# A new order of every engine's steps: the first MLP rows and the taps of k change places

## The chip, the cores and the metric

The kernel runs on one core of one Trainium2 chip. Its time is the device time of one execution in microseconds. Each kernel is run several times, and the median is given with the lowest and highest.

The core has five engines with a queue each, and an engine works through its own queue in order: TensorE (PE, matmuls and transposes into PSUM; PEld is its weight load), VectorE (DVE), ScalarE (ACT), GpSimd (POOL) and SyncE (SP), which issues all DMAs here. They wait for each other through semaphores.

## The reference

The inputs are bf16, with S = 2048 rows and D = 640 columns. The row x = `q` goes through two branches, which a gate mixes:

```
g = sigmoid((x * gate_w).sum(-1))

# branch A: a short convolution along the rows (4 taps), then a long one (FFT of length 2S)
k_shift[s] = sum_t k[s - 3 + t] * shift_k[:, 3 - t]
kv = k_shift * v
y  = irfft(rfft(kv padded to 2S) * rfft(ssm_k padded to 2S))[:S]
a  = x * (y + kv * ssm_D)

# branch B: an MLP that shifts quarters of its hidden columns along the rows, and a second MLP
h  = gelu(layernorm(x) @ w1)                      # 640 -> 640
hs = four column quarters of h, shifted by +1, -1, +2, -2 rows, @ w2
x1 = x + hs
b  = x1 + gelu(layernorm(x1) @ w3) @ w4           # 640 -> 1536 -> 640

out = g * a + (1 - g) * b
```

## The kernel before, in words

Row s lies in partition s // 16 at place s % 16, so each of the 16 places t1 is a tile of 128 rows. Rows are loaded in four quarters c of four places each.

**Branch A.** The taps of the short convolution are matmuls (`tap`, line 534): k is needed transposed (KT, channels on partitions), and a tap step multiplies slices of KT with diagonal matrices DG (line 494, built from `shift_k`) into PSUM. There are ten tap steps: `tap.0` to `tap.4` make places 0 to 7 for the five column blocks, `tap.5` to `tap.9` places 8 to 15. A tap step takes two PSUM buffers, and each half is multiplied with v in place (KV), either by VectorE from PSUM (line 548) or by a ScalarE copy (line 542) and then VectorE (line 545). So a tap needs the quarters of k and of v of its half; the first half also needs the last three places of quarter 3 turned by a partition (KW, `k_wrap`).
A quarter of k reaches KT in one of two ways, chosen in `k_load`: loaded plainly (line 507) and transposed by TensorE in 20 pieces (line 562) with copies out of PSUM by ScalarE (line 320) or VectorE (line 322), or brought by a transposing DMA on SP (line 503, the letter D).
The long convolution is a four-step Fourier transform: `step1` (lines 369 and 372) transforms KV, and the filter HT0 that `h_transpose` (lines 343, 346) makes, in eight column blocks each; copies go through a staging tile to DRAM (S_x, S_h, line 384). `gather` (line 391) reads them back in another layout, `step2` (line 413) makes the spectra XS and hs, `product` (lines 434 to 442, VectorE) multiplies them, `step3` (line 456) starts the inverse, and its copies gs go to DRAM (S_g, line 466). `gin` (line 480) reads them back, and `step4` (line 817) ends the inverse and multiplies with q and the gate (lines 821 to 831).

**Branch B.** `x_stats` (lines 620 to 636) takes mean and variance, on VectorE or ScalarE by a letter; `x_norm` (lines 603, 605) normalises; `x_turn` transposes the result, by TensorE (line 562) or by a DMA (line 593); `mlp1` (line 651) is the product with w1, its GELU (line 654) leaves PSUM into HT, and `h_shift` shifts rows. `w2` (line 728) and line 730 make x1, and line 733 its squares; `x1_norm` normalises again and transposes by DMA (line 755); `w3` (line 776), its GELU (line 781), `w4` (line 794) and line 796 end the branch. `scale_x1` (lines 300 and 302) multiplies x1 with 1 - g.

**What sets the order.** Nothing is scheduled by the compiler. `ORDER` is one long list, written out in the source, of some thousand entries `step.arguments:part`; `emit` calls them one after the other, and each part appends its instructions to the queues of its engines. A string such as `AAVVA` in an entry says, part by part, whether ScalarE (A) or VectorE (V) takes the work that either can do; D stands for a DMA transpose. Buffers come from rings of fixed size: four PSUM buffers for taps, transposes and the Fourier steps (psc), two for the MLPs (psm), four for rows in SBUF (tag row), two for transposed rows (tag xt). An instruction waits where its buffer's last reader has not finished. A DMA also waits until the eighth DMA before it has landed, since eight semaphores go round (an X load, ninth or tenth in the queue, waits for the first or second).

Line numbers below line 833 differ by three between the two kernels, because the list is three lines shorter; all lines named here lie above it.

Of the kernel before, what the change touches and what calls it, by code (L numbers as in the profile page):

```python
# [41 lines left out]
def kernel(  # L42
# [760 lines left out]
    def step4(t1, ev):  # L803
# [26 lines left out]
        def total():  # L830
# [5 lines left out]
        "open.L1.left:0 open.A2.right:0 kv_alloc:0 load_x0.0:0 consts0:0 load_x0.1:0 k_load.1.A:0 consts0:1 "  # L836
        "k_load.3.A:0 f1_table:0 load_cj:0 k_load.2.A:0 load_x.1:0 f4_table:0 v_load.3:0 f1_table:1 v_load.2:0 "
        "load_x.3:0 x_stats.0.VVVA:0 f4_table:1 x_stats.0.VVVA:1 load_w1:0 k_load.1.A:1 f1_table:2 x_stats.0.VVVA:2 "
        "x_stats.0.VVVA:3 z_cols:0 k_load.1.A:3 k_load.1.A:2 load_gw:0 k_load.1.A:5 x_stats.0.VVVA:4 k_load.3.A:1 "
        "load_h.4:0 k_load.1.A:4 kv_consts:0 k_load.3.A:3 k_load.1.A:6 k_load.3.A:2 k_load.3.A:5 k_load.0.D:0 "  # L840
        "k_load.2.A:1 k_load.3.A:4 k_load.2.A:3 k_load.3.A:6 x_stats.0.VVVA:5 k_load.2.A:5 k_load.2.A:2 "
        "x_stats.1.VVVV:0 x_stats.0.VVVA:6 k_load.2.A:4 x_stats.1.VVVV:1 k_load.2.A:6 tap.5.VA:0 x_norm.0.AVVV:0 "
        "x_norm.0.AVVV:1 x_norm.0.AVVV:2 tap.6.AA:0 x_norm.0.AVVV:3 tap.5.VA:2 tap.5.VA:1 tap.5.VA:3 tap.7.AV:0 "
        "tap.6.AA:1 x_stats.1.VVVV:2 tap.6.AA:3 tap.8.AA:0 tap.7.AV:1 tap.6.AA:2 tap.6.AA:4 tap.7.AV:2 x_turn.0.A:0 "
        "tap.7.AV:3 tap.8.AA:1 tap.8.AA:3 x_stats.1.VVVV:3 x_turn.0.A:4 x_turn.0.A:2 x_turn.0.A:1 tap.8.AA:2 "
        "x_turn.0.A:3 tap.8.AA:4 tap.9.AV:0 x_stats.1.VVVV:4 w1_mixed:0 x_stats.1.VVVV:5 x_stats.3.VVAA:0 x_turn.0.A:5 "
        "step1.KV.6.VVAVA:0 x_stats.3.VVAA:1 step1.KV.6.VVAVA:2 mlp1.0.0:0 tap.9.AV:3 tap.9.AV:1 load_h.0:0 "
        "x_norm.1.VVAV:0 x_stats.3.VVAA:2 x_norm.1.VVAV:1 v_load.1:0 tap.9.AV:2 x_norm.1.VVAV:2 v_load.0:0 "
        "x_norm.1.VVAV:3 step1.KV.6.VVAVA:1 load_x.2:0 step1.KV.6.VVAVA:4 mlp1.0.0:1 step1.KV.6.VVAVA:6 load_h.1:0 "
        "mlp1.0.1:0 step1.KV.6.VVAVA:3 d_fold:0 step1.KV.6.VVAVA:7 load_h.2:0 x_stats.3.VVAA:3 step1.KV.6.VVAVA:5 "  # L850
        "step1.KV.6.VVAVA:8 k_wrap:0 x_turn.1.V:0 x_stats.3.VVAA:4 x_turn.1.V:2 x_turn.1.V:1 step1.KV.6.VVAVA:9 "
        "x_turn.1.V:4 mlp1.0.2:0 x_stats.3.VVAA:5 x_turn.1.V:3 step1.KV.6.VVAVA:10 x_turn.1.V:5 mlp1.0.1:1 "
        "step1.KV.7.VVAVA:0 x_stats.3.VVAA:6 step1.KV.7.VVAVA:2 step1.KV.7.VVAVA:4 step1.KV.7.VVAVA:6 mlp1.0.2:1 "
        "step1.KV.7.VVAVA:1 mlp1.1.2:0 x_stats.3.VVAA:7 step1.KV.7.VVAVA:5 step1.KV.7.VVAVA:3 step1.KV.7.VVAVA:7 "
        "step1.KV.7.VVAVA:8 mlp1.1.2:1 mlp1.1.1:0 x_norm.3.VAVV:0 x_norm.3.VAVV:1 x_norm.3.VAVV:2 x_norm.3.VAVV:3 "
        "step1.KV.7.VVAVA:9 x_stats.2.VVAA:0 x_turn.3.D:0 x_stats.2.VVAA:1 tap.3.VA:0 mlp1.1.1:1 h_shift.0:0 "
        "h_shift.0:1 tap.4.VA:0 x_stats.2.VVAA:2 x_stats.2.VVAA:3 tap.3.VA:2 mlp1.1.0:0 x_stats.2.VVAA:4 tap.3.VA:1 "
        "tap.4.VA:2 tap.3.VA:3 x_stats.2.VVAA:5 tap.4.VA:1 tap.4.VA:3 tap.2.AV:0 step1.KV.7.VVAVA:10 mlp1.1.0:1 "
        "x_stats.2.VVAA:6 load_h.3:0 h_shift.0:2 tap.1.AA:0 tap.2.AV:1 x_stats.2.VVAA:7 tap.2.AV:3 tap.0.VV:0 "
        "tap.1.AA:1 tap.2.AV:2 tap.1.AA:3 x_norm.2.VAAV:0 step1.KV.4.AVAVV:0 x_norm.2.VAAV:1 tap.1.AA:2 "  # L860
        "step1.KV.4.AVAVV:2 tap.1.AA:4 mlp1.3.1:0 tap.0.VV:1 x_norm.2.VAAV:2 x_norm.2.VAAV:3 step1.KV.4.AVAVV:1 "
        "tap.0.VV:2 x_turn.2.D:0 step1.KV.4.AVAVV:3 step1.KV.4.AVAVV:4 mlp1.3.1:1 step1.KV.4.AVAVV:6 h_shift.0:3 "
        "step1.KV.4.AVAVV:8 step1.KV.1.AAAAV:0 mlp1.3.2:0 step1.KV.4.AVAVV:5 step1.KV.4.AVAVV:7 step1.KV.1.AAAAV:1 "
        "step1.KV.4.AVAVV:9 step1.KV.1.AAAAV:2 mlp1.3.2:1 step1.KV.1.AAAAV:4 h_shift.1:0 step1.KV.1.AAAAV:8 "
        "step1.KV.4.AVAVV:10 step1.KV.1.AAAAV:6 step1.KV.1.AAAAV:3 h_shift.1:1 mlp1.3.0:0 step1.KV.1.AAAAV:9 "
        "step1.KV.1.AAAAV:5 step1.KV.1.AAAAV:7 h_shift.1:2 h_shift.1:3 step1.KV.1.AAAAV:10 load_w2:0 step1.KV.3.AVAAV:0 "
        "mlp1.3.0:1 step1.KV.3.AVAAV:2 step1.KV.3.AVAAV:4 step1.KV.3.AVAAV:3 step1.KV.3.AVAAV:6 mlp1.2.1:0 "
        "step1.KV.3.AVAAV:1 h_shift.3:0 step1.KV.3.AVAAV:5 step1.KV.3.AVAAV:7 h_shift.3:1 h_shift.3:2 "
        "step1.KV.3.AVAAV:8 mlp1.2.1:1 z_cols:1 step1.KV.2.VVAVV:0 h_shift.3:3 z_rows:0 step1.KV.3.AVAAV:9 z_cols:2 "
        "step1.KV.2.VVAVV:1 step1.KV.3.AVAAV:10 step1.KV.2.VVAVV:2 z_rows:1 step1.KV.2.VVAVV:6 step1.KV.2.VVAVV:3 "  # L870
        "step1.KV.2.VVAVV:8 mlp1.2.2:0 step1.KV.2.VVAVV:7 step1.KV.2.VVAVV:9 step1.KV.5.AAAAA:0 step1.KV.5.AAAAA:4 "
# [12 lines left out]
        "step1.HT0.4.AAAAA:5 step1.HT0.4.AAAAA:7 step1.HT0.4.AAAAA:8 step1.HT0.6.VAVAV:0 step1.HT0.6.VAVAV:2 "
        "step1.HT0.4.AAAAA:9 w2.11:1 step1.HT0.6.VAVAV:4 i_tables:4 step1.HT0.4.AAAAA:10 step1.HT0.6.VAVAV:6 "
        "step1.HT0.6.VAVAV:1 w2.8:0 step1.HT0.6.VAVAV:5 step1.HT0.6.VAVAV:3 step1.HT0.6.VAVAV:7 w2.9:1 "
        "step1.HT0.6.VAVAV:8 w2.0:2 step1.HT0.5.AVAAA:0 w2.8:1 step1.HT0.5.AVAAA:2 step1.HT0.5.AVAAA:4 "
        "step1.HT0.5.AVAAA:1 w2.5:0 step1.HT0.6.VAVAV:9 step1.HT0.5.AVAAA:5 step1.HT0.5.AVAAA:3 w2.1:2 "
        "step1.HT0.6.VAVAV:10 step1.HT0.5.AVAAA:6 w2.5:1 step1.HT0.5.AVAAA:8 t2_table:2 step1.HT0.7.AAVAV:0 "
        "step1.HT0.7.AAVAV:2 w2.15:0 t2_table:3 t2_table:4 step1.HT0.5.AVAAA:7 step1.HT0.5.AVAAA:9 step1.HT0.7.AAVAV:1 "  # L890
        "step1.HT0.7.AAVAV:4 step1.HT0.5.AVAAA:10 step1.HT0.7.AAVAV:6 w2.14:0 step1.HT0.7.AAVAV:3 step1.HT0.7.AAVAV:5 "
        "step1.HT0.7.AAVAV:7 w2.15:1 w2.3:2 step1.HT0.7.AAVAV:8 step1.HT0.3.AVVVA:0 w2.14:1 t2_table:5 "
        "step1.HT0.3.AVVVA:2 step1.HT0.3.AVVVA:4 w2.13:0 step1.HT0.7.AAVAV:9 step1.HT0.3.AVVVA:1 step1.HT0.3.AVVVA:3 "
        "step1.HT0.7.AAVAV:10 w2.2:2 step1.HT0.3.AVVVA:5 step1.HT0.3.AVVVA:6 step1.HT0.3.AVVVA:8 table.1.AV:0 "
# [89 lines left out]
                 f1_table=f1_table, t2_table=t2_table, i_tables=i_tables, f4_table=f4_table, kv_alloc=kv_alloc, k_load=k_load, k_wrap=k_wrap, v_load=v_load, tap=tap,  # L984
                 kv_consts=kv_consts, mlp1=mlp1, load_h=load_h, h_transpose=h_transpose,
# [50 lines left out]
```

## Time and profile before

| | |
|---|---|
| median of 7 runs | 242.51 us |
| lowest and highest | 241.05 and 243.67 us |
| the profiled execution | 242.49 us |
| its span in the profile | 240.7 us |
| TensorE busy | 222.8 us (93%) |
| VectorE busy | 209.3 us (87%) |
| ScalarE busy | 175.9 us (73%) |
| GpSimd busy | 11.1 us (5%) |
| moved by DMA | 57.05 MB, mean 237 GB/s |
| granted TensorE clock | 1.00 |

The span goes from the first to the last recorded instruction; the time has about 1.8 us more around it. The busy time of TensorE counts a matmul from its start to its modelled end, and matmuls overlap, so it is above the time for which the array is needed. In the stages below, each row gives busy us and the number of instructions of each engine; in the chain of waits, each row is a piece of the path that ended last.

### The profile page before, as it was taken

Reading aid. Unit: us, or ns where it says so; the run is one execution under the profiler, and the core shown is the slowest. Engines: PE = TensorE matmul, PEld = TensorE weight load, DVE = VectorE, ACT = ScalarE, POOL = GpSimd, SP = SyncE. Lnnn points to the kernel's source line nnn. Section 1 sums busy time; section 2 is a strip of 40 time slices with the busy share of each in tenths; the row PEclk is TensorE's granted clock in tenths of the full one; section 3 lists DMA queues with packets and bytes.
Section 4 is the critical chain, followed back from the end, with each engine's and each line's share of the span. In section 5 each row is a group of like instructions: output and inputs, shape, how many; then the busy total and the mean of one; then the engine's idle time right before and its main releaser. Section 6 shows DMA issues by size and latency. Waiting matters only on the chain.

```text
span 240.7 us, 5159 instructions
## 1 busy us (share of the span) xinstructions
PE 222.8 (93%) x2024; PEld 121.5 (50%) x2041; DVE 209.3 (87%) x428; ACT 175.9 (73%) x300; POOL 11.1 (5%) x26
## 2 busy tenths in 40 slices
PE   0879999999999999999999999999999999999973
PEld 0765556444865555434444444555434456456551
DVE  7999989977889999769999999999999997157795
ACT  4999999769899999999959866836568632336430
POOL 1022012000000020004200000000000000000000
PEclk9999999999999999999999999999999999999999
DMA  7999999885869959986999837986500475589813
GB/s 245 388 378 171 376 348 263 219 281 213 241 216 376 407 205 231 319 326 188 275 284 237 250 137 228 191 277 228 169 4 1 152 222 200 163 293 326 277 65 109
DMA packets 48390, 57.05 MB, mean 237 GB/s; under 512 B 23017, under 2 KB 40170, under 8 KB 48110
## 3 DMA queue, kind: packets, MB, share of 16 engines
q1 hardware_dynamic: 48366, 56.72, 77.1%
q8 instruction: 16, 0.26, 0.4%
q14 instruction: 8, 0.07, 0.1%
HBM read 33.77 MB, written 18.36 MB: 217 GB/s over the span
## 4 chain that ended last, share of the span: by engine, by line
PE 37%; DVE 34%; ACT 12%; DMA 8%; SPq 5%; issue 3%; DVEq 0%
PE ps L776 13%; PE ps L794 8%; PE psm L651 4%; DVE p L436 4%; DVE p L434 4%; SPq L503 4%; DMA X<-in_A_q_dram 4%; ACT HT L346 3%; DVE X L796 3%; DVE hs L442 3%; DVE hs L440 3%; DVE hs L438 3%; PE ps L369 3%; PE psw L728 3%; DMA q<-in_A_q_dram 2%
## 5 line engine op out<-in xcount | busy, mean ns | idle before, releaser
L794 PE MATMUL ps<-W,gt 128*128 128x128 bf16 (+1 forms) x372 | 55.9, 297 | 0.8 <-issue 0.3
L776 PE MATMUL ps<-x1t,W 128*128 128x512 bf16 x240 | 55.3, 379 | 0.7 <-DVE X L796 0.7
L794 PEld LDWEIGHTS <-gt 128*128 128x128 bf16 x384 | 29.6, 98 | 24.1 <-issue 2.8
L781 ACT ACTIVATE gt<-ps 128x1024 bf16<-128x1024 f32 x24 | 24.8, 1034 | 20.5 <-PE ps L776 20.5
L776 PEld LDWEIGHTS <-W 128*128 128x128 bf16 x240 | 22.5, 98 | 27.4 <-issue 3.4
L322 DVE CAST stg<-ps 128x512 bf16<-128x512 f32 x35 | 22.8, 686 | 3.1 <-PE ps L369 2.9
L320 ACT CAST stg<-ps 128x512 bf16<-128x512 f32 x45 | 25.0, 637 | 0.7 <-PE ps L369 0.7
L320 ACT CAST gs<-ps 128x512 bf16<-128x512 f32 x33 | 17.4, 600 | 11.0 <-PE ps L456 10.0
L651 PE MATMUL psm<-xt,WA 128*128 128x512 bf16 x100 | 23.5, 379 | 0.0
L728 PE MATMUL psw<-WA,HT 128*128 128x512 bf16 (+1 forms) x111 | 20.4, 295 | 0.2
L320 ACT CAST hs<-ps 128x512 bf16<-128x512 f32 x31 | 16.5, 616 | 2.5 <-PE ps L413 2.4
L821 ACT ACTIVATE y<-ps,GS 128x320 bf16<-128x320 f32 x17 | 8.0, 525 | 11.5 <-PE ps L817 11.1
L322 DVE CAST XS<-ps 128x512 bf16<-128x512 f32 x21 | 13.4, 684 | 3.4 <-PE ps L413 3.3
L827 DVE SCALAR_TENSOR_TENSOR q<-ps,GS,q 128x320 bf16<-128x320 f32 x15 | 7.8, 547 | 9.7 <-PE ps L817 8.0
L651 PEld LDWEIGHTS <-WA 128*128 128x128 bf16 x100 | 9.6, 98 | 11.1 <-issue 0.6
L728 PEld LDWEIGHTS <-HT 128*128 128x128 bf16 x116 | 10.0, 98 | 10.0 <-issue 0.7
L796 DVE SCALAR_TENSOR_TENSOR X<-ps,OMG,X 128x640 bf16<-128x640 f32 x16 | 14.0, 879 | 0.2
L730 DVE SCALAR_TENSOR_TENSOR X<-psw,X 128x640 bf16<-128x640 f32 x16 | 12.9, 821 | 1.0 <-PE psw L728 1.0
L413 PE MATMUL ps<-ax,CMP 64*32 64x512 bf16 (+3 forms) x512 | 13.4, 300 | 0.1
L733 ACT ACTIVATE jk<-X 128x640 bf16<-128x640 bf16 x16 | 13.3, 834 | 0.0
L654 ACT ACTIVATE HT<-psm 128x1024 bf16<-128x1024 f32 (+1 forms) x12 | 10.5, 882 | 3.4 <-PE psm L651 3.4
L320 ACT CAST XS<-ps 128x512 bf16<-128x512 f32 x19 | 10.5, 608 | 3.1 <-PE ps L413 3.1
(142 smaller groups left out, 375.9 us busy)
## 6 DMA issues: line engine op xcount, KB each, us to landing
S_x<-stg SPq DMA_DIRECT2D x8, 640.0 KB, 4.1
ax<-S_x SPq DMA_DIRECT2D x8, 640.0 KB, 5.1
S_h<-stg SPq DMA_DIRECT2D x8, 640.0 KB, 8.3
ax<-S_h SPq DMA_DIRECT2D x8, 640.0 KB, 4.4
S_g<-gs SPq DMA_DIRECT2D x8, 640.0 KB, 3.2
W<-in_B_w_dram SPq DMA_DIRECT2D x2, 1920.0 KB
KV<-in_A_v_dram SPq DMA_DIRECT2D x4, 640.0 KB
q<-in_A_q_dram SPq DMA_DIRECT2D x4, 640.0 KB
```

Of the source, the lines that this page charges most:

```text
L320: A.copy(out=dst, in_=src)
L322: V.tensor_copy(out=dst, in_=src)
L413: PE.matmul(ps[j][q:q + 32, lo - 512 * u:hi - 512 * u], lhsT=CMP[r, 0, 8 * b + 2 * i + o, c, :], rhs=ax[i // 2][r, 2 * (i % 2) + o, lo - i ...
L651: PE.matmul(ps[:, v, :].rearrange("p (a b) -> p a b", a=4), lhsT=W1N[:, k, 160 * f:160 * f + P] if f < 4 else W1M[:, k, :], rhs=xt[:, :, k ...
L654: A.activation(out=st["HT"][:, 4 * c:4 * c + 4, 2 * u:2 * u + nf, :].rearrange("p t f b -> p f t b"), in_=ps[:].rearrange("p f (t b) -> p ...
L728: PE.matmul(ps[:, o:o + w], lhsT=h_tile(f, t1), rhs=W2P[:, f, o:o + w], start=(f == 0), stop=(f == 4))
L730: V.scalar_tensor_tensor(out=X1[:, t1, :], in0=ps[:], scalar=1.0, in1=X[:, t1, :], op0=ALU.mult, op1=ALU.add, accum_out=S12[:, 0, t1:t1 + 1])
L733: A.activation(out=jk[:], in_=X1[:, t1, :], func=ACT.Square, accum_out=S12[:, 1, t1:t1 + 1])
L776: PE.matmul(ps[:, u, :].rearrange("p (a b) -> p a b", a=4), lhsT=st["W3"][:, k, f * P:(f + 1) * P], rhs=xt[:, :, k, :], start=(k == 0), st ...
L781: A.activation(out=gt[:, 2 * (fp % 2):2 * (fp % 2) + 2, :], in_=ps[:], func=ACT.Gelu_apprx_tanh)
L794: PE.matmul(ps[:, o:o + w], lhsT=st["gt", c, f // 4][:, f % 4, i * P:(i + 1) * P], rhs=st["W4"][:, f, o:o + w], start=(f == 0), stop=(f == ...
L796: V.scalar_tensor_tensor(out=X1[:, t1, :], in0=ps[:], scalar=OMG[:, t1:t1 + 1], in1=X1[:, t1, :], op0=ALU.mult, op1=ALU.add)
```

## The change

Only the list `ORDER` changes: 1002 entries become 993. Every function stays as it is, and so do the sizes and the number of the buffers.

- The start is rearranged. Before, three quarters of k are loaded and transposed by TensorE first (`k_load.1.A`, `.3.A`, `.2.A`), four tap steps of the second half follow, and the first MLP step (`mlp1.0.0`) comes after them. Now three quarters of x are loaded first, both of the first x quarters are normalised and turned, and `mlp1.0.0`, `mlp1.0.1` and `mlp1.1.1` stand among the first taps. All ten taps come before the first `step1` entry; before, `step1.KV.6` and `.7` stood between the two halves of the taps.
- Quarter 1 of k is now brought by the transposing DMA (`k_load.1.D`) instead of TensorE, beside quarter 0, which was already. TensorE issues 20 transposes fewer (2 x 20 remain for k instead of 3 x 20), SP issues two transposes of k instead of one and two plain k loads instead of three. Quarter 2 leaves PSUM on VectorE (`k_load.2.V`) instead of ScalarE, and `x_turn.1` on ScalarE instead of VectorE.
- SP's queue starts x, x, x, k, k, x, v, w1, shift_k, k transposed, v, x, v, ssm_k, k transposed, gate_w, v; before it started x, x, k, k, shift_k, k, x, v, v, x, w1, gate_w, ssm_k, k transposed, ssm_k, v, v, x.
- The later steps change their sequence too (the column blocks in `step1`, the rows in `w2`, the slots in `product` and `step3`, the rows in `step4`), and many A and V letters change. In all, VectorE gives eight of its 22 normalisations and two of its ten scalings to ScalarE; it takes five more hs copies, one more gs copy and three KT copies, and three fewer XS copies, four fewer step1 copies and three fewer xt copies. `load_w4` moves from between the last `step1.HT0` entries to behind `gather.h.7`, and `gather.x.6` from before the filter's step1 to behind it.

The head of the list, up to the last tap, in both orders:

```diff
-        "open.L1.left:0 open.A2.right:0 kv_alloc:0 load_x0.0:0 consts0:0 load_x0.1:0 k_load.1.A:0 consts0:1 "
-        "k_load.3.A:0 f1_table:0 load_cj:0 k_load.2.A:0 load_x.1:0 f4_table:0 v_load.3:0 f1_table:1 v_load.2:0 "
-        "load_x.3:0 x_stats.0.VVVA:0 f4_table:1 x_stats.0.VVVA:1 load_w1:0 k_load.1.A:1 f1_table:2 x_stats.0.VVVA:2 "
-        "x_stats.0.VVVA:3 z_cols:0 k_load.1.A:3 k_load.1.A:2 load_gw:0 k_load.1.A:5 x_stats.0.VVVA:4 k_load.3.A:1 "
-        "load_h.4:0 k_load.1.A:4 kv_consts:0 k_load.3.A:3 k_load.1.A:6 k_load.3.A:2 k_load.3.A:5 k_load.0.D:0 "
-        "k_load.2.A:1 k_load.3.A:4 k_load.2.A:3 k_load.3.A:6 x_stats.0.VVVA:5 k_load.2.A:5 k_load.2.A:2 "
-        "x_stats.1.VVVV:0 x_stats.0.VVVA:6 k_load.2.A:4 x_stats.1.VVVV:1 k_load.2.A:6 tap.5.VA:0 x_norm.0.AVVV:0 "
...
...
+        "open.L1.left:0 open.A2.right:0 kv_alloc:0 load_x0.0:0 consts0:0 load_x0.1:0 load_x.1:0 consts0:1 k_load.3.A:0 "
+        "f1_table:0 k_load.2.V:0 load_x.2:0 v_load.0:0 f4_table:0 load_w1:0 f1_table:1 load_cj:0 k_load.1.D:0 z_cols:0 "
+        "x_stats.0.VVAA:0 f4_table:1 x_stats.0.VVAA:1 x_stats.1.VVVV:0 x_stats.0.VVAA:2 x_stats.0.VVAA:3 "
+        "x_stats.0.VVAA:4 k_load.3.A:1 x_stats.1.VVVV:1 x_stats.0.VVAA:5 k_load.3.A:3 k_load.3.A:2 x_stats.0.VVAA:6 "
+        "k_load.3.A:5 k_load.2.V:1 k_load.3.A:4 x_stats.1.VVVV:2 x_stats.0.VVAA:7 k_load.2.V:3 k_load.3.A:6 "
+        "x_stats.1.VVVV:3 x_norm.0.AVAA:0 k_load.2.V:5 x_norm.0.AVAA:1 x_norm.0.AVAA:2 x_stats.1.VVVV:4 x_turn.0.A:0 "
+        "k_load.2.V:2 x_stats.1.VVVV:5 x_norm.0.AVAA:3 k_load.2.V:4 k_load.2.V:6 x_turn.0.A:1 x_turn.0.A:2 f1_table:2 "
+        "x_turn.0.A:4 x_norm.1.VVVV:0 x_turn.0.A:3 x_norm.1.VVVV:1 x_norm.1.VVVV:2 x_turn.1.A:0 w1_mixed:0 x_turn.0.A:5 "
+        "x_norm.1.VVVV:3 kv_consts:0 x_turn.1.A:1 x_turn.1.A:2 mlp1.0.0:0 x_turn.1.A:3 v_load.2:0 load_x.3:0 v_load.3:0 "
+        "load_h.0:0 x_stats.2.VVVV:0 x_turn.1.A:4 k_load.0.D:0 mlp1.0.0:1 mlp1.0.1:0 x_stats.2.VVVV:1 x_stats.2.VVVV:2 "
+        "tap.7.VA:0 x_turn.1.A:5 mlp1.0.1:1 x_stats.2.VVVV:3 tap.5.VA:0 tap.7.VA:2 k_wrap:0 mlp1.1.1:0 x_stats.2.VVVV:4 "
+        "tap.5.VA:2 x_stats.3.VVAA:0 x_stats.2.VVVV:5 x_stats.3.VVAA:1 tap.7.VA:1 x_stats.3.VVAA:2 tap.7.VA:3 "
+        "tap.9.AV:0 tap.5.VA:1 mlp1.1.1:1 tap.5.VA:3 x_norm.2.VAVA:0 x_norm.2.VAVA:1 tap.6.VV:0 x_norm.2.VAVA:2 "
+        "load_gw:0 tap.9.AV:3 x_norm.2.VAVA:3 v_load.1:0 mlp1.1.0:0 x_stats.3.VVAA:3 load_h.2:0 tap.9.AV:1 x_turn.2.D:0 "
+        "x_stats.3.VVAA:4 tap.9.AV:2 tap.6.VV:1 x_stats.3.VVAA:5 tap.6.VV:2 tap.8.VA:0 mlp1.1.0:1 x_stats.3.VVAA:6 "
+        "x_stats.3.VVAA:7 tap.3.VA:0 tap.8.VA:1 tap.8.VA:2 tap.1.AV:0 tap.8.VA:3 tap.3.VA:2 tap.3.VA:1 tap.3.VA:3 "
+        "tap.2.AV:0 tap.1.AV:1 tap.1.AV:3 tap.1.AV:2 load_w2:0 tap.0.AA:0 tap.2.AV:1 tap.2.AV:3 load_h.1:0 tap.2.AV:2 "
+        "tap.4.VA:0 load_h.4:0 tap.0.AA:1 d_fold:0 tap.0.AA:3 tap.0.AA:2 step1.KV.4.AAVVA:0 x_norm.3.AVAV:0 "
...
```

## The prediction

> **What bounds the kernel now.** I read the busy time of the engines by stage first, because the mean over the span (TensorE 93%, VectorE 87%, ScalarE 73%) hides which engine is full where. Columns: stretch, its length, then busy us of TensorE (PE), its weight loads, VectorE (DVE), ScalarE (ACT), GpSimd, the granted TensorE clock, the DMA share, GB/s.
>
> ```profile
> 0.00:5.00 5.00, 0.00 (x0) 0.00 (x0) 3.49 (x24) 1.69 (x2) 1.17 (x10) 1.00 0.64 218
> 5.00:10.00 5.00, 3.64 (x39) 3.51 (x39) 4.68 (x14) 4.70 (x10) 0.00 (x0) 1.00 0.99 372
> 10.00:15.00 5.00, 3.38 (x60) 2.58 (x59) 4.86 (x16) 5.00 (x7) 1.22 (x2) 1.00 1.02 421
> ...
> 75.00:80.00 5.00, 4.88 (x32) 2.51 (x30) 4.58 (x10) 5.00 (x11) 0.00 (x0) 1.00 1.04 394
> ...
> 160.00:170.00 10.00, 9.89 (x108) 5.05 (x108) 9.82 (x10) 4.72 (x9) 0.00 (x0) 1.00 0.64 215
> ...
> 200.00:210.00 10.00, 10.00 (x63) 5.13 (x60) 3.69 (x5) 3.61 (x5) 0.00 (x0) 1.00 0.47 158
> ```
>
> TensorE is idle at the start and full afterwards; ScalarE is full beside it around 75, VectorE around 165. A busy TensorE is not yet one at its rate, so I made a ruler: start-to-start times from the timeline and the chain. Ten 128x512 matmuls take 2.16 us (one MLP step), a w2 step 1.37, a w4 step 3.26, a tap 0.94 (two from 33.26 to 35.13), a step1 piece 0.22, a step2 piece 0.31, a step4 half 0.27. Summed over the order this gives 219.2 us of TensorE work before. Set against real times: the last tap ends at 40.9 with 29.9 done, so **11.0 lost**; the first w3 matmul starts at 97.5 with 84.2 done, 13.3 lost; the first product at 120.6 with 107.6 done, 13.0 lost. Between the first and last product (120.6 to 199.9) the ruler says 75.4 and the clock 79.3: there VectorE decides. So the start loses most, and whatever is lost there is not made up: the stage up to 97 is full on two engines, the products are full on VectorE, and the end is TensorE again.
>
> Next the chain of waits at the start, then SyncE's (SP) queue:
>
> ```profile
> 6.36 1.05 PE pst L562 x8
> 7.43 4.75 ACT KT L320 x7
> ...
> 14.11 8.69 SPq L503
> 22.86 0.57 SPq L152
> ...
> 24.42 8.48 DMA X<-in_A_q_dram
> ```
>
> Line 503 is the transposing DMA that brings a quarter of k straight into KT. Nothing behind it on SP is issued for 8.69 us, and the load of X behind it lands at 32.9. Two others, with little queued ahead of them, hold SP for less:
>
> ```profile
> 32.49 5.25 SPq L593 DMA_TRANSPOSE xt<-xn  x1
> ...
> 42.49 3.08 SPq L593 DMA_TRANSPOSE xt<-xn  x1
> ```
>
> My reading: a hold lasts until the queue ahead has drained, plus about 3.1 us. Test: ahead of line 503 lie 6.6 MB; by the two-microsecond rates they have moved by 20.0, and 20.0 + 3.1 is 23.1, where 22.8 was measured.
>
> **The change, part by part.**
>
> *Removed.* One of three quarters of k no longer goes through TensorE. Twenty transposes fall away; 56 took from 6.36 to 11.4, 0.088 each, so -1.8 us of TensorE (219.2 to 217.5). Its copies, 2 x 0.92 + 0.50, leave ScalarE.
>
> *Added.* A second line-503 transpose (quarter 1), tenth on SP, behind x rows 0 to 11, two quarters of k, one of v, and w1: 4.75 MB. By the rates above (1.09 MB by 5 us, 2.95 by 10, 5.06 by 15) these have moved by 14.3. SP is free 3.1 later, at 17.4 to 17.8. Behind it wait v2, x3, v3, h0 and the other transpose (quarter 0), then v1.
> v3: the X load above, with 2.49 MB from the end of the hold to its own last byte, landed 10.1 after that end (22.8 to 32.9). v3 closes 1.97 MB; 0.52 MB less at 0.39 MB/us is 1.3 less, so 17.6 + 8.8 = **26.4**.
> Second transpose: the 2.49 MB have drained at 26.0, SP is free at 29.1, v1 lands 5 later, **34.1**, up to 35.5 if the 640 small pieces of gate_w ahead of it cost a microsecond.
>
> *Moved: the start.* x comes first, so the first k quarter lands at 7.9 instead of 6.3 (0.66 MB more ahead at 0.41). TensorE does 40 k transposes to 11.4 and waits for the norms: ScalarE's four statistics (0.85 each, from 5.7) end at 9.1, GpSimd's power 1.25 after VectorE's six small steps at 11.5, three normalisations to 14.2, transposes' copies to 16.7. The first MLP step starts at about 16.8, not 21.5, and three run to 25.5 with two taps between them. The third tap needs a PSUM pair that VectorE frees by multiplying with v, and v3 has not landed before 26.4. VectorE itself reaches that multiplication at 25.7 (mask product 2.83 to 19.5, four statistics 4.2, wrap and small steps 1.0, one more 1.1), so the DMA adds 0.7 to VectorE's own order. From 26.4 VectorE needs 7.4 for the taps of the second half with what lies between (0.94 a tap, 1.2 for the one without ScalarE, two normalisations 0.74, one statistics 1.06, small steps 0.6): 33.8. Then quarter 0's taps wait for v1 at 34.1 to 35.5, three of them 2.8 us, and the last tap's matmuls end at **38.5** (37.2 if no DMA is late, 39.5 at the other end). Ruler there: 23.8 done, so **14.7 lost against 11.0**.
>
> *Moved: the stage to the first w3.* ScalarE has 59.3 us of instructions from its first step1 copy to the table load for w3 (before 53.1, from 42.0 to 99.9; eight more step1 copies at 0.48, two half GELUs at 0.49, two normalisations at 0.82, one XS copy at 0.49, one scaling of 0.78 less); TensorE has 58.9 from its last tap, VectorE 50.9 (48.6) to its last step1 copy. Before, TensorE lost 2.3 here. Now two engines are equally full; I take 3.0, bounds 0 and 5. First w3 matmul: 82.7 + 14.7 + 3.0 = 100.4, against 97.5.
> Queues in this part: the w4 load is moved behind the last spectrum stores, which landed 9.6 late behind it, and the h gathers gain that; they have cover, since 13.9 us of TensorE work (16.0 before) lie between the last step1 and the first h step2. One x gather, in turn, now stands behind these stores: 8.0 of TensorE work cover 0.5 + 5.1 + about 2; 0 to 1 us, inside the bounds.
>
> *Moved: the rest.* VectorE and ScalarE swap evacuations: by the rows VectorE -3.8 us in all, ScalarE +4.3, mostly eight normalisations (0.44 on VectorE, 0.95 on ScalarE). To the first product TensorE has 23.2 instead of 23.4. Products: VectorE's work between the first and last is 78.4 instead of 77.4 (seven hs copies for five, nine line-796 additions for eight, two scalings for four), so +1.0. Behind the last product TensorE has 35.1 instead of 36.2: -1.1. The wait for the last q load stays: before, VectorE had 4.4 us to do between its issue and first use and idled 1.7; now it has 4.0. SP's stores keep their places near the end. Sum behind the first w3: -0.3.
>
> **Sum:** +2.9 - 0.3 = +2.6. The profiled execution took 242.49 with a span of 240.7, so 245.1 with a span of 243.3; it stands at the median of the runs (242.51), so I predict **245.1 us**.
>
> One rule of the Trainium skill speaks further against this change. The row first: the 128-column transposes come 12 to a microsecond from 6.3 to 9.3 and 16 to a microsecond from 10.3, though the granted clock shows 1.00 throughout. TensorE: Matmul & The Clock Gate, Part 1 (The HAM clock gate) says that an array idle for a window of about 3.4 us runs its next 3.4 us at half rate. In the new order TensorE has some 2 us of work between 11.4 and 16.8; if the gate closed, the first MLP steps would last an estimated 1.7 us longer, and a sum that adds it gives 246.8. The sum above goes by the granted clock and adds nothing, and TensorE waits for v behind these steps anyway.
>
> **Rivals.**
> *A, ends faster: VectorE, not TensorE, sets the end from the taps on.* It carries the chain from 118 to 200. Its last tap product ended at 42.9 with 168.0 us of its work left; now at about 39.0 with 170.2 left: 1.7 earlier, **240.8**. It decides if TensorE makes up its lost start by 97, that is if it loses under 1 us in the step1 stage. Against it: VectorE idles 7.6 us between 45 and 100 before, so it isn't the bound there.
> *B, slower still: ScalarE bounds the step1 stage.* It idled 4.8 in it before, 4.3 of that before 62, while TensorE fed it. The same idling now puts the w3 table load at 39 + 59.3 + 4.8 = 103.1 instead of 99.9, and TensorE, with two PSUM pairs for w3, stalls on the late GELUs for another 2: 242.5 + 3.2 + 2 - 0.3 = **247.4**.
> *C, the order does nothing on balance:* no DMA is late (last tap at 37.2) and the stage loses 2.3 as before: first w3 at 82.7 + 13.4 + 2.3 = 98.4, +0.9 - 0.3, **243.1**; with 1 us less lost, 242.1.
>
> **Chances.** Forecast (243.8 to 246.5) 0.40, A 0.27, B 0.15, C 0.18. The range of 8 in 10 reaches to A and past B: 240.2 to 248.3; the forecast's own is 243.8 to 246.5. A measurement here can tell about 0.5% from no change, 1.2 us: faster is A, 0.27; within it is C, 0.18; slower is the forecast and B, 0.55.
>
> **What will show it.** SP's line 503 twice, the first ending near 17.6, the second near 29; first MLP matmul near 17; TensorE waiting for VectorE's KV products near 26 and 34; the last tap near 38.5 and the first w3 matmul near 100. If the first hold ends by 12, my rule of the drained queue is wrong and A or C gains. If ScalarE is still at step1 copies at 103, it is B. If the products take much less than 80 us, VectorE wasn't their bound.

## The result, and the profile after

The changed kernel takes **245.45 us** (median of 27 runs, 243.70 to 248.53); the kernel before, run beside it, takes 243.66 us (median of 64 runs, 241.05 to 247.67). The ratio is **1.0081, 95% interval 1.0062 to 1.0100**: slower by 1.5 to 2.4 us. The ratio leaves out the few runs in a slower state of the chip, such as the one of 248.53. The profiled execution of the changed kernel took 245.66 us with a span of 243.9, against 242.49 and 240.7 before.

The same views in the same order. First busy time by stretch (columns as in the prediction: stretch, length, TensorE, weight loads, VectorE, ScalarE, GpSimd, granted clock, DMA share, GB/s):

```profile
5.00:10.00 5.00, 1.50 (x15) 1.50 (x16) 4.24 (x15) 4.22 (x11) 0.00 (x0) 1.00 1.00 395
10.00:15.00 5.00, 4.53 (x48) 3.87 (x46) 4.88 (x20) 4.97 (x7) 2.43 (x4) 1.00 1.25 359
...
25.00:30.00 5.00, 3.75 (x53) 2.50 (x51) 4.26 (x10) 4.75 (x9) 0.95 (x2) 1.00 1.21 179
...
75.00:80.00 5.00, 4.95 (x33) 2.79 (x33) 4.68 (x11) 4.98 (x11) 0.00 (x0) 1.00 1.03 383
...
115.00:120.00 5.00, 4.00 (x47) 1.85 (x48) 4.79 (x13) 5.00 (x8) 1.30 (x3) 1.00 1.08 363
160.00:170.00 10.00, 9.95 (x90) 5.38 (x89) 9.78 (x10) 5.17 (x10) 0.00 (x0) 1.00 0.89 298
```

The same stretch from 115 to 120 before:

```profile
115.00:120.00 5.00, 4.79 (x67) 2.50 (x67) 4.60 (x14) 4.76 (x9) 1.22 (x2) 1.00 1.29 281
```

TensorE now has holes at 5 to 10 (1.50 us busy, 3.64 before), at 25 to 30 (3.75, 5.00 before) and at 115 to 120 (4.00, 4.79 before). Its timeline names the last two, and one between them (start, length, line, in brackets the idle time ahead and who ended it):

```profile
27.58 1.97 PE L534 MATMUL psk<-DG,KT 64*128 64x256 bf16 x43 [1.25 <-DVE KV L548]
...
51.63 2.32 PE L651 MATMUL psm<-xt,WA 128*128 128x512 bf16 x10 [0.94 <-DMA xt<-xn]
...
118.82 2.75 PE L794 MATMUL ps<-W,gt 128*128 128x512 bf16 x11 [0.91 <-DMA W<-in_B_w_dram]
```

The chain of waits at the start is now SyncE's queue and one load of v, up to the taps of the first half:

```profile
5.36 11.46 SPq L503
...
19.19 9.05 SPq L503
...
28.92 5.31 DMA KV<-in_A_v_dram
...
34.31 0.70 DVE KV L548
...
35.05 2.90 PE psk L534 x48
```

The two transposing DMAs of k hold SP to 16.8 and 28.2, the last v lands at 34.2, and the taps end at 38.0.

Later I profiled both kernels once more (`b_again`, `a_again`, on two different chips of the same kind). Marks in us, all read from the timeline, where the last tap of before ends at 41.0 (the prediction's 40.9 was the chain's row):

| | before | after | b_again | a_again |
|---|---|---|---|---|
| first k transposes | 6.36 | 8.50 | 8.14 | 9.71 |
| last tap ends | 41.0 | 38.0 | 42.3 | 38.0 |
| first w3 matmul | 97.5 | 100.3 | 98.9 | 100.0 |
| first product | 120.6 | 123.9 | 121.9 | 123.7 |
| last product ends | 199.8 | 204.4 | 201.2 | 204.1 |
| last line 796 ends | 237.9 | 241.0 | 239.5 | 240.6 |
| span | 240.7 | 243.9 | 242.3 | 243.4 |

Differences, first pair and second pair: last tap -3.0 and -4.3; last tap to first w3 (56.5 before) +5.8 and +5.4; to the first product +0.6 both times; products (79.3) +1.2 both times; behind them (38.0, 38.3) -1.4 and -1.9. Sums, from unrounded marks, +3.2 and +1.1. The differences of all stages but the first repeat within 0.5; the start's do not.

### The profile page after: what moved, and what is told of

Read it like the earlier page. It is cut to its first block, busy times and chain, and to the rows that moved or that the text cites. A ratio compares the mean times of both kernels' runs of the same rounds, so it can differ in the third digit from the quotient of the medians.

```text
span 243.9 us, 5101 instructions
## 1 busy us (share of the span) xinstructions
PE 222.9 (91%) x2004; PEld 121.2 (50%) x2021; DVE 207.0 (85%) x416; ACT 180.4 (74%) x302; POOL 11.0 (4%) x26
## 4 chain that ended last, share of the span: by engine, by line
DVE 37%; ACT 21%; PE 16%; SPq 11%; DMA 8%; issue 5%; DVEq 0%; ACTq 0%
SPq L503 8%; ACT stg L320 5%; DVE p L436 5%; DVE hs L438 5%; DVE X L796 4%; PE ps L776 4%; DVE hs L442 4%; DVE hs L440 4%; DMA xt<-xn 4%; ACT jk L733 4%; DVE p L434 4%; PE ps L794 3%; ACT gt L781 2%; DMA KV<-in_A_v_dram 2%; DVE hs L322 2%
## 5 line engine op out<-in xcount | busy, mean ns | idle before, releaser
L794 PE MATMUL ps<-W,gt 128*128 128x128 bf16 (+1 forms) x372 | 55.3, 297 | 1.7 <-DMA W<-in_B_w_dram 0.9
L320 ACT CAST stg<-ps 128x512 bf16<-128x512 f32 x49 | 27.2, 644 | 0.3 <-PE ps L369 0.3
L322 DVE CAST stg<-ps 128x512 bf16<-128x512 f32 x31 | 20.4, 686 | 7.3 <-PE ps L369 3.8
L728 PE MATMUL psw<-WA,HT 128*128 128x512 bf16 (+1 forms) x112 | 21.0, 296 | 0.3
L320 ACT CAST hs<-ps 128x512 bf16<-128x512 f32 x26 | 14.0, 625 | 2.1 <-PE ps L413 2.0
L320 ACT CAST XS<-ps 128x512 bf16<-128x512 f32 x22 | 12.0, 606 | 4.7 <-PE ps L413 4.7
L322 DVE CAST XS<-ps 128x512 bf16<-128x512 f32 x18 | 11.6, 684 | 2.0 <-PE ps L413 1.9
L733 ACT ACTIVATE jk<-X 128x640 bf16<-128x640 bf16 x16 | 12.6, 790 | 0.0
```

What stands on the lines that cost most here:

```text
L320: A.copy(out=dst, in_=src)
L322: V.tensor_copy(out=dst, in_=src)
L728: PE.matmul(ps[:, o:o + w], lhsT=h_tile(f, t1), rhs=W2P[:, f, o:o + w], start=(f == 0), stop=(f == 4))
L733: A.activation(out=jk[:], in_=X1[:, t1, :], func=ACT.Square, accum_out=S12[:, 1, t1:t1 + 1])
L794: PE.matmul(ps[:, o:o + w], lhsT=st["gt", c, f // 4][:, f % 4, i * P:(i + 1) * P], rhs=st["W4"][:, f, o:o + w], start=(f == 0), stop=(f == ...
```

## The experiments

Ratios are to the kernel before, run on the same chip.

**Joining the lists.** Which part of the list holds the loss? Two kernels take one list up to its last tap and the rest from the other.

```diff
 "... tap.4.VA:1 tap.4.VA:2 tap.4.VA:3"
-"step1.KV.4.AAVVA:4 step1.KV.4.AAVVA:3 step1.KV.4.AAVVA:6 step1.KV.4.AAVVA:5 ..."
+"mlp1.0.2:1 step1.KV.6.VVAVA:0 step1.KV.6.VVAVA:2 step1.KV.6.VVAVA:1 ..."
```

`a_start_b_rest` (new start, old rest). 

> The new list up to its last tap (without the entries of step1.KV.4 and x_norm.3), then what is left in the old list's sequence and with the old letters. Theory (the start is what costs: 3.1 us more lost on TensorE at the last tap, 1.8 us fewer transposes): last tap near 38, first w3 at 98.8 (before 97.5, after 100.3), and 1.3 us slower than before, ratio 1.005. Rival 1 (the start costs nothing, the later lists do): ratio 0.998 to 1.001. Rival 2 (the whole loss at the first w3, 2.7 us, comes from the start): ratio 1.011.

Measured: 253.62 us, ratio 1.0415 (1.0372 to 1.0458). None of the three. TensorE stood still for x quarter 3, which the new start turns last and the old rest needs first:

```profile
51.40 4.26 PE L651 MATMUL psm<-xt,WA 128*128 128x512 bf16 x10 [7.91 <-DMA xt<-xn]
```

The last tap came at 37.9 as expected, but the join added 7.9 us of standing still, and the ten matmuls after it took 4.26 instead of 2.32. Of the whole change it tells nothing; behind the fault, first w3 to first product (23.1) and the products (79.3) are those of the kernel before.

`b_start_a_rest` (old start, new rest), the mirror:

```diff
 "... tap.0.VV:1 tap.0.VV:2"
-"x_turn.2.D:0 step1.KV.4.AVAVV:3 step1.KV.4.AVAVV:4 mlp1.3.1:1 ..."
+"x_norm.2.VAVA:0 x_norm.2.VAVA:1 x_norm.2.VAVA:2 x_norm.2.VAVA:3 x_turn.2.D:0 load_w2:0 ..."
```

> The mirror: the old list up to its last tap (without step1.KV.4, x_norm.2 and mlp1.3.1), then what is left in the new list's sequence and letters, the late w4 load and the new tail among it. Theory: start as before (last tap near 41), the step1 stage loses 1.1 us more than before, w3 to first product +0.6, products +1.2, behind the last product -1.4: 1.5 us slower than before, ratio 1.006. Rival 1 (the later lists hold the whole loss): ratio 1.008 or more, like the changed kernel. Rival 2 (the start holds it all): ratio 1.000 to 1.002.

Measured: 252.69 us, 1.0392 (1.0350 to 1.0433): the same fault, 4.83 us of waiting for quarter 2. Behind it the stages are clean: first w3 to first product 23.7, products 80.5, behind them 36.5, each as in the changed kernel.

So I made both again with the first-MLP steps of quarters 2 and 3 changed over in the rest, and `h_shift` set behind the steps it reads.

```diff
-"... mlp1.3.1:0 ... mlp1.3.2:0 ... mlp1.2.1:0 ..."
+"... mlp1.2.1:0 ... mlp1.2.2:0 ... mlp1.3.1:0 ..."
```

`e_newstart_oldrest`. 

> The new list up to its last tap (without step1.KV.4 and x_norm.3), then what is left in the old list's sequence and letters, with the first-MLP steps of the quarters 2 and 3 of x changed over, since the new start turns quarter 2 first. The first join of this kind stood still for 7.9 us for quarter 3 and then ran ten matmuls at half rate; without these 10 us it is at 243.6. Theory (the start costs +3.1 -1.8 = +1.3 us): ratio to before 1.003 to 1.007. Rival 1 (the start costs nothing, the later lists do): 0.997 to 1.001. Rival 2 (all of the +2.7 at the first w3 comes from the start): 1.011.

`e_oldstart_newrest`. 

> The mirror, changed over in the same way: the old start, then what is left in the new sequence. Theory (the later lists cost +1.1 in the step1 stage, +0.6 to the first product, +1.2 in the products, -1.4 behind): +0.5 to +1.5 us, ratio 1.002 to 1.006. Rival 1 (they hold the whole loss): 1.008 or more. Rival 2 (the start holds it all): 0.998 to 1.002.

Measured: 1.0171 (1.0110 to 1.0232) and 1.0133 (1.0087 to 1.0180). Both medians lie above the changed kernel's ratio (the second one's interval overlaps it), so the parts do not add up, and none of my theories fits both: the first run lies at or above the upper end of what was expected, where the start holds the whole loss, the second where the later lists hold it. The stages say where. The new start with the old rest ends its taps at 37.8 but takes 65.5 us to the first w3 (62.0 with the new rest): all eight blocks of step1 are left behind the taps, where the old list by itself leaves six, and the old letters were not made for the extra copies; TensorE waits there for staging copies and shifted rows in six places, 3.3 us in all. The old start with the new rest takes 58.1 us to the first w3 (56.5 with its own), then 23.7, 80.5 and 37.0. Each rest goes best with its own start. What does not depend on the start is shown: +0.6 to the first product and +1.2 in the products belong to the new rest.

**The new tail alone.** `b_prod_a_tail`:

```diff
 "... product.4:3 product.4:4 w4.11:1 w4.9:1 w4.11:2"
-"step3.4.AAAVV:0 step3.4.AAAVV:2 w4.9:2 step3.4.AAAVV:1 ..."
+"w4.9:2 w4.8:0 w4.8:1 w4.8:2 step3.4.AAAAA:0 step3.4.AAAAA:2 ..."
```

> The old list up to its last product entry, then what is left in the new list's sequence. Theory (the new tail is shorter by its own order, 36.6 against 38.0 us behind the last product, because the last q load is in time): 1.2 us faster than before, ratio 0.995, and VectorE's idle 1.7 us ahead of the last rows of q is gone. Rival (the tail was shorter because less work was left for it when the products ended later): ratio 1.000.

Measured: 1.0059 (1.0039 to 1.0079), slower. Behind the last product it takes 38.5, as before (38.0 and 38.3), not 36.6. The wait for q is down to 0.4, but the join puts a whole w4 step ahead of step3.4, and TensorE waits 0.62 for VectorE and 0.49 for the S_g read instead. My -1.4 as a property of the new tail alone is not confirmed. The rival's 1.000 does not hold either: the kernel is slower by about 1.4 us, and the tail does not account for it. Against `b_again` its profile differs by 0.4 us at the first transposes (8.54) and by 0.2 in the tail; why its runs are slower stays open.

**Quarter 1 of k by TensorE again.** `a_k1_tensor`:

```diff
-load_cj:0 k_load.1.D:0 z_cols:0
+load_cj:0 k_load.1.A:0 z_cols:0
...
-mlp1.0.0:0 x_turn.1.A:3 v_load.2:0
+mlp1.0.0:0 k_load.1.A:1 x_turn.1.A:3 k_load.1.A:3 k_load.1.A:2 v_load.2:0
...
-mlp1.0.0:1 mlp1.0.1:0
+mlp1.0.0:1 k_load.1.A:5 k_load.1.A:4 k_load.1.A:6 mlp1.0.1:0
```

> The new list with quarter 1 of k loaded plainly and transposed by TensorE in 20 pieces (copies by ScalarE) instead of by the first transposing DMA. Theory (the drained queue holds SP until 16.8 and makes v late; VectorE's own order is next, 0.7 us behind): SP is never held ahead of v2, x3 and v3, v3 lands by 21, the last tap ends near 37.2 instead of 37.9, TensorE has 1.8 us more work, of which it had idle time to take: 0.5 to 1.5 us faster than the changed kernel, 1.002 to 1.006 of before. Rival 1 (late v is the start's whole loss): taps follow v3 from 21 on, last tap by 34, 3 us faster than the changed kernel, ratio 0.996. Rival 2 (ScalarE bounds the step1 stage, so the start doesn't matter, and three more copies cost it 2.3 us): slower than the changed kernel, ratio 1.010 or more.

Measured: 246.10 us, 1.0100 (1.0057 to 1.0144): no gain on the changed kernel. The ratio is the one of rival 2, but the stage from the last tap to the first w3 is no longer than in the changed kernel (61.3 against 62.0 to 62.3), so the step1 stage is not where it loses. v3 is issued at 13.5 instead of 18.0 (the plain load of quarter 1 itself holds SP for 5.68) and TensorE does not wait for it, but the last tap ends at 39.9. Two rows of SP and one of TensorE:

```profile
6.83 5.68 SPq L507 DMA_DIRECT2D kn<-in_A_k_dram  x1
...
14.85 12.72 SPq L503 DMA_TRANSPOSE KT<-in_A_k_dram  x1
```

```profile
25.40 2.13 PE L534 MATMUL psk<-DG,KT 64*128 64x256 bf16 x43 [1.07 <-ACT KT L320]
```

The remaining transpose holds SP to 27.6 (28.2 with two), and the taps wait for ScalarE's copies of k instead of for v. So taking the second transposing DMA away does not make the start earlier: the 20 transposes and their copies, which come in its place, end it 1.9 us later here. How late it would be without either, no run shows.

**Two DMA waits taken out.** `a_waits_out`:

```diff
-load_w2:0 tap.0.AA:0 tap.2.AV:1 tap.2.AV:3 load_h.1:0 tap.2.AV:2 tap.4.VA:0 load_h.4:0 tap.0.AA:1
+tap.0.AA:0 tap.2.AV:1 tap.2.AV:3 tap.2.AV:2 tap.4.VA:0 tap.0.AA:1
...
-x_turn.3.D:0 mlp1.1.2:0
+x_turn.3.D:0 load_w2:0 load_h.1:0 load_h.4:0 mlp1.1.2:0
...
-gather.x.6:0
+load_w4:0 gather.x.6:0
...
-load_w4:0 w2.12:2
+w2.12:2
```

> The new list with two waits of TensorE for DMAs taken away by the order of SP alone: the w2 load and two filter loads go behind the transposing DMA of x quarter 3 (0.94 us of waiting at 51.6), and the w4 load goes ahead of the three gathers it stood behind (0.91 us at 118.8). Theory (a wait of TensorE ahead of the first w3 is lost for good, the other one counts too since TensorE is full up to the products): the transpose holds SP for 3 to 4.5 us instead of 7.4, both waits are gone, 1.8 us faster than the changed kernel, ratio to before 1.000 to 1.002. Rival (between 92.7 and 123.9 the chain of waits runs on ScalarE alone, so the w4 wait covers time in which ScalarE was behind anyway): only the first counts, 0.9 us, ratio 1.004. Rival 2 (ScalarE is the bound of both): no gain, ratio 1.008.

Measured: 252.31 us, 1.0373 (1.0323 to 1.0423), far outside. Both waits are gone, and two others are there, one of them longer. SP first (the w4 load, then the gathers), then TensorE:

```profile
42.73 4.21 SPq L593 DMA_TRANSPOSE xt<-xn  x1
...
102.32 0.55 SPq L180 DMA_DIRECT2D W<-in_B_w_dram  x1
102.93 1.36 SPq L391 DMA_DIRECT2D ax<-S_x  x1
106.15 15.43 SPq L391 DMA_DIRECT2D ax<-S_h  x4
```

```profile
113.38 0.63 PE L413 MATMUL ps<-ax,CMP 64*32 64x512 bf16 x24 [4.73 <-DMA ax<-S_x]
113.94 4.02 PE L776 MATMUL ps<-x1t,W 128*128 128x512 bf16 x10
```

The x gather behind the w4 load came 4.7 us late, and first w3 to first product took 29.6 instead of 23.7. So w4 cannot simply be loaded ahead of the x gather: in one queue, the gather is then late. The transposing DMA held SP for 4.21 instead of about 7, as the rule of the drained queue says. But last tap to first w3 stayed at 61.9: at 59.0 TensorE waits 1.06 us for a staging copy, as in the next run, which shows why.

**One wait and ScalarE's letters.** `a_turn_letters` has the first of the two moves alone, and five instructions moved from ScalarE to VectorE:

```diff
-x1_norm.2.AVVA scale_x1.3.A scale_x1.8.A scale_x1.11.A
+x1_norm.2.VVVV scale_x1.3.V scale_x1.8.V scale_x1.11.V
```

> The new list with the w2 load and two filter loads behind the transposing DMA of x quarter 3 (the w4 load stays), and with five ScalarE instructions between the first w3 and the first product given to VectorE: two normalisations of x1_norm.2 (0.82 each) and three scalings (0.72 each), 3.8 us off ScalarE and 2.1 onto VectorE, which idles 3.1 us between 105 and 115. Theory (the DMA wait of 0.94 is lost for good; ScalarE alone is the chain from 92.7 to the first product): no wait at 51.6, last tap to first w3 0.5 to 0.9 us shorter than 62.4, first w3 to first product 22.5 to 23.1 instead of 23.7; 1 to 1.8 us faster than the changed kernel. Rival (TensorE and VectorE decide there, the w4 load the rest): 23.7 or longer, 0.5 us faster or no gain.

Measured: 245.61 us, 1.0077 (1.0049 to 1.0105): no gain. The rival's number holds, but not for its reason. The first row is TensorE's, the second ScalarE's, the third TensorE's again:

```profile
58.70 0.38 PE L372 MATMUL ps<-KV,F 128*128 128x256 bf16 x2 [1.08 <-ACT stg L320]
...
58.06 1.07 ACT L320 CAST stg<-ps 128x512 bf16<-128x512 f32 x2 [1.35 <-DMA S_x<-stg]
...
118.71 2.75 PE L794 MATMUL ps<-W,gt 128*128 128x512 bf16 x12 [1.36 <-DMA W<-in_B_w_dram]
```

The 0.9 us won at 51 is given back seven microseconds later. ScalarE is not full there; its staging copy waits 1.35 us for a store of S_x that has to empty the tile first. In the changed kernel that store is issued at 49.69 and lands at 53.75. Here it is issued at 49.05, right behind the three loads that I had moved, and lands at 57.96. So the move took one DMA out of TensorE's way and put another there, and last tap to first w3 is 62.0, as without it. Behind the first w3 it is as the rival says: ScalarE had less to do, and TensorE only waited longer for w4 (1.36 instead of 0.67 in `a_again`); first w3 to first product was 23.85.

**The products.** `a_prod_light` and `b_prod_light` give copies of spectra in the product stage to ScalarE. The diff of the second; the first changes x.1, h.0 (but for its leading V), h.1, x.2 and h.2 likewise:

```diff
-step2.x.1.AVVAAAAAVA step2.h.1.AAAAVAAAVA step2.x.2.VAAVAAAAAV step2.h.2.AVAVAAAAVA
+step2.x.1.AAAAAAAAAA step2.h.1.AAAAAAAAAA step2.x.2.AAAAAAAAAA step2.h.2.AAAAAAAAAA
```

> The new list with twelve copies out of PSUM of the product stage (step2.x.1, h.0, h.1, x.2 and h.2) on ScalarE instead of VectorE: 8.2 us off VectorE, 5.9 onto ScalarE, which idles 30 us there. Theory (VectorE bounds the products, 80.5 us for 75.4 of TensorE work): products 76 to 78 us, 2 to 3.5 us faster than the changed kernel, ratio to before 0.994 to 1.000. Rival (ScalarE's copies queue behind its GELUs, free PSUM later, and TensorE waits for them): products 80 us or more, ratio 1.006 or more.

> The same on the old list: eleven copies (step2.x.1, h.1, x.2, h.2) on ScalarE, 7.5 us off VectorE. Theory: products 76 to 77.5 instead of 79.3 us, 2 to 3 us faster than before, ratio 0.987 to 0.993, faster than both kernels. Rival: products 79 us or more, ratio 0.998 or more.

Measured: 245.11 us, 1.0057 (1.0028 to 1.0085), and **242.84 us, 0.9961 (0.9934 to 0.9987)**. The products took 79.7 instead of 80.5, and 78.15 instead of 79.3. That is 0.8 us of the 2.5 to 4.5 expected and 1.1 of 1.8 to 3.3: the direction is the theory's, the size much smaller. Neither whole time lies where the theory or its rival put it. (By the diff `a_prod_light` moves eleven copies, not twelve.) Beside `a_again` on the same chip (1.0030) its whole time shows no gain. Two stretches of `b_again`, then of `b_prod_light`:

```profile
140.00:160.00 20.00, 19.41 (x162) 9.37 (x162) 19.65 (x18) 13.51 (x22) 0.00 (x0) 1.00 0.74 196
180.00:200.00 20.00, 19.56 (x128) 9.59 (x129) 19.58 (x17) 12.02 (x21) 0.00 (x0) 1.00 0.35 116
```

```profile
140.00:160.00 20.00, 20.00 (x166) 9.57 (x165) 18.44 (x16) 15.33 (x26) 0.00 (x0) 1.00 0.76 217
180.00:200.00 20.00, 19.73 (x133) 9.90 (x132) 16.02 (x13) 13.05 (x23) 0.00 (x0) 1.00 0.36 117
```

VectorE was the full one, and with 3.6 us less to do in the last stretch it is not; TensorE, busy for 19.4 and 19.6 of 20 us before, is full or nearly so instead. So VectorE did bound the products, with TensorE about 1.1 us behind. In the new list the gain is smaller still, and there ScalarE is now busy for 20.00 of the 20 us from 140 to 160. The old list with the lighter VectorE is the fastest kernel here: it beats both. Not all of that need come from the letters: its profile is also 1.6 us shorter behind the last product than `b_again` (36.7 against 38.3), where the last load of q lands sooner.

**The two kernels again.** The edit is none. `b_again`: 

> The kernel before, unchanged, profiled once more on this chip, because a kernel with the same start had its first transposes at 8.54 instead of 6.36 us, on the chip of the runs above. If the chip or the run sets that, this profile shows the first k transposes later than 6.4 too, and every later mark (last tap 40.9, first w3 97.5, first product 120.6, last product 199.8) later by about the same 1.5 to 2 us; if not, it repeats the marks within 0.3 us.

`a_again`: 

> The changed kernel, unchanged, on this chip. The old kernel's second profile had its first k transposes 1.8 us later (8.14 for 6.36) and its last tap at 42.1 for 40.9. Theory (the old start waits for k from the first microsecond on, the new one mostly for v behind the held queue and for VectorE, so a late first load costs the new one less): first k transposes 1 to 1.5 us later than 8.50, last tap later by under 0.8, first w3 at 100.3 to 101.2, ratio 1.006 to 1.010. Rival (it costs both the same): last tap at 39.2, first w3 at 101.6.

Measured: `b_again` 244.10 us in its one run, beside 243.94 for the kernel before; `a_again` 244.38 us, 1.0030 (0.9996 to 1.0064), so on that chip the change is not clear of none. Of its theory the last tap held (38.0), while the first w3 (100.0) and the ratio came out below their ranges. The first transposes, of the first and then of the second:

```profile
8.14 5.76 PE L562 MATMUL pst<-IDB,kn 128*128 128x128 bf16 x60 [8.14 <-DMA kn<-in_A_k_dram]
```

```profile
9.71 4.07 PE L562 MATMUL pst<-IDB,kn 128*128 128x128 bf16 x40 [9.71 <-DMA kn<-in_A_k_dram]
```

The old start follows its first load of k one for one: in `b_again` and four other kernels with this start the load came at 8.1 to 9.0 and the last tap ended 34.2 later each time (34.6 in the profile before, with the load at 6.4; there the chain runs over the transposing DMA of the prediction instead). The new start does not follow it: in seven profiles the load came between 8.5 and 10.0, and the last tap ended between 37.75 and 38.5. The first k does not set it. In three of the seven the chain to the last tap is the one shown above, SP's two holds and the last v. In the others it runs over the v of the second half and VectorE's products (in `a_again` that v lands at 26.9 and VectorE carries the chain from there to 34.1), or over VectorE's work from the load of x on. The prediction had the two ways 0.3 us apart (33.8 and 34.1), and they end together here too. The new one loses at the first w3, then, 2.7 us against the profile before, 1.1 against `b_again`, and 0.3 against `b_prod_light` (99.7, its list as before up to there, on the chip of `a_again`).

## Why the prediction was right, and where it was not

(In the prediction's text, "x rows 0 to 11" means the places 0 to 11, and "mask product" the product that makes DG.) The direction and the size held: +2.6 was forecast, 1.5 to 2.4 measured, 3.2 between the two profiles it compares. That 245.1 lies so near 245.45 is in part luck: the base of seven runs was 1.15 us below the median of all 64, and +2.6 is 0.6 above the measured 2.0. Its steps:

- **The start's marks** held: first hold to 16.8 (forecast 17.4 to 17.8), second to 28.2 (29.1), first MLP matmul at 17.3 (16.8), v for the second half at 26.8 (26.4), v1 at 34.2 (34.1), last tap at 38.0 (38.5; with v1 at 34.1 to 35.5 the written terms make 36.9 to 38.3, and the product with v between them, 0.70 in the chain above, is not among them). The rule of the drained queue carried it, and a third and a fourth hold agree with it: 7.17 and 7.39 us with loads queued ahead, the fourth 4.21 with three of them moved behind it. The traces show it directly too: the ssm_k load ahead of the second hold lands at 28.09 and the hold ends at 28.25; in `b_again` that load lands at 23.28 and the hold ends at 23.32.
- **The start's price** is the term that failed: 14.7 lost against 11.0. The new side was near (14.2). The old side was read from one profile in which k landed at 6.4; in the other five profiles with the old start it lands at 8.1 to 9.0, and at 8.14 the old start loses 12.4. The 1.8 us between 14.2 and 12.4 are, by the ruler, just the 1.8 us of transposes that the change removes. So the start costs 1.3 net against the early profile, nothing against `b_again`, and gains a little where k is later still. I had also put the late v down to a DMA that could be spared; with transposes by TensorE in its place the taps ended later (39.9).
- **Step1 stage**: 3.0 lost against 2.3 was forecast; 3.1 to 3.4 against 2.2 measured. The size held. Of the reason, two full engines, the part from 60 to 100 is shown: TensorE is busy for 39.47 and ScalarE for 39.92 of these 40 us in the changed kernel. Ahead of 60 there are waits of TensorE that were not foreseen, 0.94 for x quarter 3 at 51.6 and 0.45 just before it, and they count: in the six profiles with both the new start and the new rest the stage takes 61.3 to 62.3 us, and less TensorE's waits in it (1.0 to 1.8 in sum) it takes 60.3 to 60.5 in each.
- **To the first product**: -0.2 forecast, +0.6 measured. The prediction priced this stage by TensorE's work alone, and in the new list ScalarE is its bound. The stage before, after, and in `b_start_a_rest`:

```profile
97.50:120.50 23.00, 22.79 (x282) 9.89 (x283) 19.07 (x47) 22.23 (x40) 3.75 (x6) 1.00 0.91 269
```

```profile
100.30:123.90 23.60, 22.24 (x278) 9.67 (x275) 19.51 (x45) 23.57 (x40) 3.76 (x6) 1.00 0.95 313
```

```profile
107.10:130.70 23.60, 23.25 (x282) 10.00 (x279) 19.35 (x45) 23.57 (x40) 3.75 (x6) 1.00 0.97 316
```

  ScalarE has five normalisations there instead of one, and is busy for 23.57 of 23.60 us. The prediction also booked the later w4 load as a gain for the h gathers and did not ask when w4 itself lands: it is issued at 106.7 instead of 96.8, and TensorE waits 0.91 for it. But this wait is not the price: it is 0.67 in `a_again` and nothing in `b_start_a_rest`, and the stage takes 23.7 in all three. It sets the stage only once ScalarE has less to do (`a_turn_letters`).
- **Products**: +1.0 forecast, +1.2 measured, for the reason given (VectorE).
- **Behind the last product**: -1.1 forecast from less TensorE work, -1.4 and -1.9 measured, but the reason is not settled. "The wait for the last q load stays" was wrong. The load lands 4.5 us after its issue in the new kernel (227.55 to 232.08) and 6.0 and 6.3 in the old one (1.7 and 2.0 of VectorE idle); in `b_prod_light`, old tail, it took 4.7 and that tail took 36.7 against 36.5 to 36.6. So nearly all of the -1.4 is q in time. It goes with the new rest as a whole: the tail takes 36.5 to 37.3 in the eight profiles that have it, and 37.7 to 38.3 in four of the five with the old tail. Why q lands sooner there stays open.
- **The Trainium skill's rule of the clock gate**, which would have added an estimated 1.7 us, did not apply: the first MLP step took 2.16 us start to start and the granted clock stayed at 1.00. Of the two signs the step's time decides, since the column gives 1.00 in the slow stretch of the start too. The row that the prediction set beside it was misread: the transposes start 107 ns apart from 6.4 to 9.5 (9 to 10 to a microsecond, not 12) and 56 ns apart from there on.

Of the rivals, B's mechanism was there (ScalarE as the chain from 92.7 to the first product; w3 table load at 103.7, forecast 103.1) without its price, since the stage ahead lost no more than forecast. A did not happen: VectorE idled 5.2 us at 50 to 60 and 3.2 at 105 to 115, and the last tap's earlier end was used up before the products.

## What to carry to other kernels

Read the first load's landing in more than one profile before pricing a change of the start: here it moves by 2 us, and one order follows it one for one while the other does not. Before you take away a wait by moving a DMA, ask what then stands behind the moved ones in the queue: here both moves made another transfer late, a gather once and a store once, by as much as was won or more. Before you relieve an engine, ask what is late by the same amount beside it, as w4 was beside ScalarE. Only relief of the engine that was alone in front (VectorE in the products) gained, and only as far as the next engine. Where a list was planned as a whole, joined halves show the stages that do not depend on the start, not the price of each half.

## What the runs showed of the hardware

- After long standing still in the middle of the kernel TensorE ran at half rate, and the granted clock shows it, not only the matmuls. In `a_start_b_rest` it waited 7.9 us to 51.4:

```profile
48.00:51.40 3.40, 0.00 (x0) 0.00 (x0) 0.00 (x0) 0.00 (x0) 0.00 (x0) 0.58 1.00 255
51.40:53.50 2.10, 2.10 (x6) 0.72 (x6) 0.00 (x0) 0.00 (x0) 0.00 (x0) 0.50 1.01 319
53.50:56.00 2.50, 2.50 (x9) 1.01 (x8) 0.00 (x0) 0.30 (x1) 0.00 (x0) 0.63 0.24 97
```

  Ten matmuls then took some 4.1 us instead of 2.16. After 4.7 us (`a_waits_out`) ten took 3.95, after 4.8 us (`b_start_a_rest`) five took 2.1 instead of 1.08. After waits of up to 1.4 us no such row was seen. The Trainium skill's page TensorE: Matmul & The Clock Gate, Part 1 (The HAM clock gate) says that an idle window of about 3.4 us halves the rate; these three waits agree with it. The wait of 4.7 us so cost another 1.8 in the ten matmuls behind it, the one of 4.8 us another 1.0 in its five.
- At the start the clock column does not show the slow stretch. The first transposes start 107 ns apart for 3.2 to 5.4 us in all fourteen profiles, and 56 ns apart after that, while the column gives 1.00. In the changed kernel (24 in 2.5 us):

```profile
8.50:11.00 2.50, 2.50 (x24) 2.50 (x25) 2.36 (x13) 2.05 (x4) 0.32 (x1) 1.00 1.01 416
```

- A plain load can hold SP too. The tenth DMA in `a_k1_tensor` was issued for 5.68 us (line 507 at 6.83), and in all six profiles of the old start the ssm_k load ahead of line 503 for 4.98 to 5.11 (at 9.01 in the kernel before), where most take 0.3 to 1.0.
- The landing of the same k load, third on SP in the old list, differed between chips and runs by up to 2.6 us (first transposes at 6.36 to 8.99).
